# q and k of batches 4 and 5 through the DMA crossbar: a sliding-window attention with a channel mix behind it

## The chip, the core and the metric

The kernel runs on one core of one Trainium2 chip. The metric is the device time of one execution in microseconds (us); the median over several executions is given where there are several. TensorE (PE in the profile, PEld for its weight loads), VectorE (DVE), ScalarE (ACT), GpSimd (POOL) and SyncE (SP) are the core's engines. POOL and SP compute almost nothing here: they issue DMAs.

## The reference, cut to what matters

```python
# q, k, v: 8 batches x 8 heads x 576 positions x 64
scores = scale * q @ k.T                       # per batch and head
bias   = -slope[h] * abs(i - j)                # 0 <= i - j < 128, else masked
attn   = softmax(scores + bias);  a = attn @ v
x      = heads of a side by side               # 8 x 576 x 512
x_prev = x shifted down by one position
xk = mu_k * x + (1 - mu_k) * x_prev;  xr = mu_r * x + (1 - mu_r) * x_prev
k  = relu(xk @ w_k)                            # 512 -> 1024
v  = (k * k) @ w_v                             # 1024 -> 512
out = sigmoid(xr @ w_r) * v
```

## The kernel before, in words

Everything is computed in bf16 with float32 sums. Loads that cast float32 to bf16 are issued by POOL, because only its DMAs cast here.

**Attention** goes batch by batch (b = 0 to 7) and, in a batch, by pairs of heads (g = 0 to 3). For one pair, the first step is q and k with the 64 columns of a head on the partitions: the transposed form. The scores of the whole pair are twelve TensorE matmuls (L728), two ACT exponentials (L742, `at`), two DVE multiplications with a mask that holds the bias (L755). Then come 18 matmuls with v (L783, `attend`), a reciprocal and a multiplication on DVE (L789, L795, `xu`), and a transposition back into `xt`. DVE makes `dl`, `xk` and `xr` from it (L882, L889).

**The channel mix** runs over chunks of 256, 384 or 512 positions of two batches (one chunk spans two of them). A chunk has 8 groups of four matmuls with `wk_sb` (L985), each followed by a ReLU on ACT (L992) and a square on DVE or ACT (L966 and L964, `kk`). Each block of 128 positions then has four matmuls with `wr_sb` (L1003), a tanh on ACT (L1010), two times four matmuls with `wv_sb` (L1019), a product on DVE (L1024, `ot`) and a store on SP's queue (L1049).

**How q and k get transposed** depends on the batch. In all cases the parts up to position 512 go to `cb` (two buffers) and the last 64 positions to `ts`.
- Batches 0 to 2: TensorE, by a finer scheme (L1080, and L1125 and L1128 for the first half of batch 0).
- Batches 3, 4 and 5: `qk_some` takes two pairs of heads at a time: 32 TensorE transpositions of 64 by 64 blocks (L839) into two PSUM buffers of the pool `uno` (four buffers of one bank each), then four ACT copies (L698) of 128 by 512 into `qk`.
- Batches 6 and 7, the members of `XB`: eight DMA transposes on SP's queue (L537, `flip`), one for each 128 positions of q and of k, from `cb` straight into `qx`. TensorE and ACT do nothing for it. `qx` has two buffers; batch 0 uses the same memory for its staging.

The tails in `ts` go through the crossbar for batches 4 to 7 (L630), and `xu` of batches 6 and 7 goes back to `xt` through it too (L904). L839 also serves the way back of batches 1 to 5 (from `xu`).

```python
def flip(b, i, j, g):
    return dma(SPE, FLIP * RATE, FISSUE, lambda e: nc.sync.dma_start_transpose(
        out=qx_buf[xbh[b].idx][:, i, :, 128 * j:128 * j + 128],
        in_=cb_buf[ch[b].idx][:, i, j].rearrange("p h d -> p (h d)")), ...)

# in the loop over batches
if b in XB:
    hq, y = xbh[b], xbl[b]            # all eight flips of the batch
elif g % QM == 0:
    two_q[:] = qk_some(b, g, QM, prio)
```

**The order of the work** is fixed before anything runs. Each operation is a node of a plan, and `ORDER` holds, for PE, ACT and DVE, the complete list of node numbers in which the engine executes them. An engine that waits for one entry executes nothing behind it. POOL's and SP's DMAs are chained in the order in which the program makes them, except that output stores and the `xt` transposes are put among SP's transposes where the planner's clock says; that clock uses the costs in `COST`, a factor for each kind of transfer. The order in POOL's queue is, for each batch: eight loads into `cb` (four of q, four of k), two into `ts`, five of v into `vs` and `tv`.

A store waits on SP for its product on DVE; transposes behind it in the queue wait with it. A load into `cb` waits until the buffer's last reader is done: a TensorE transposition, or a DMA transpose for the batches in `XB`. `ot` has five buffers, of which the planner hands out the lowest free one.

Of the kernel before, what the change touches and what calls it, by code (L numbers as in the profile page):

```python
# [20 lines left out]

ORDER = {
    "PE": [int(x) for x in """
# [16 lines left out]
""".split()],  # L40
    "ACT": [int(x) for x in """
# [12 lines left out]
""".split()],  # L54
    "DVE": [int(x) for x in """
# [16 lines left out]
""".split()],  # L72
}

# [168 lines left out]
def kernel(  # L243
# [14 lines left out]
    B, H, S, D = q.shape  # L258
# [14 lines left out]

    PE, ACT, DVE, POOL, SPE, FAB, VIR = "PE", "ACT", "DVE", "POOL", "SP", "FAB", "VIR"
    NQ, NA, NX, NV, NC = 4, 4, 4, 2, 2
    XB = range(6, B)
    XO = range(6, B)
    X0 = 16
    NWARM = 90
# [16 lines left out]
    WAIT = 0.0  # L296
    START, BACK = 1.7, 0.25
    SKEW = {'v': 0.25, 'tv': 0.3, 'ts': 0.3}
    COST = {'first': 0.9, 'v': 1.2, 'q': 0.944, 'ts': 0.66, 'tv': 0.66, 'w': 0.88, 'run4': 1.0, 'run2': 1.03, 'flip': 1.0, 'mu': 1.0, 'x': 1.0}
    SS = ()  # L300
    OH = range(1, 6)
    QM = 2
# [108 lines left out]
    def fab(queue, us, n, lat, free=(), flip=False):  # L411
        m = max(1, round(us / 0.25))
        us *= COST.get(getattr(n, "kind", None), 1.0)
        n0, edge = n, (n, lat[0])
# [7 lines left out]
    def dma(queue, kb, issue, emit, deps=(), need=(), free=(), lat=(1.0, 0.9), flip=False, kind='x'):  # L422
        n = plan.add(queue, issue, 0.0, list(deps) + [last.get(queue)],
                     (len(plan.nodes),), emit, need)
        n.kind = 'flip' if flip else kind
        last[queue] = n
        if queue == POOL:
            if len(loads) >= 8:
                loads[-8].succ.append((n, 0.9 + BACK))
                n.left += 1  # L430
            y = fab(queue, kb / RATE, n, (START, lat[1] + SKEW.get(kind, 0.0)), free, flip)
            loads.append(y)
            return y
        return fab(queue, kb / RATE, n, lat, free, flip)
# [58 lines left out]
    def issue_t(nd):  # L493
        return 0.53 + 0.00034 * nd
# [35 lines left out]
    def full_load(b, i, h, g):  # L530
        src = (q, k)[i][b, :, 0:SM].rearrange(
            "h (r p) d -> p h r d" if b in XB else "h (p r) d -> p h r d", p=128)
        return [dma(POOL, 256, issue_t(1024), lambda e, r=r: nc.gpsimd.dma_start(  # L533
# [49 lines left out]
    for g, n in ((0, 1), (1, 1), (2, 2)):  # L583
        for i in range(2):
            x = first_load(i, g, n)
# [49 lines left out]
    def batch_load(b, what):  # L635
# [7 lines left out]
        elif what == "b":  # L643
            th[b], tl[b] = tail_load(b)
            if b in XB:
                xbh[b] = Hold("qx")
# [311 lines left out]

    n_hw = 39 + sum(4 if g in FT else 2 for g in range(3)) + 8 * len(XB) + len(XTT) + G * len(XO)
    n_split = -n_hw % 8  # L960
# [282 lines left out]
    for b in range(1, B):  # L1243
# [4 lines left out]
        for g in range(G):  # L1248
            prio = (0, b, 0, g)
            ha = Hold("at")  # L1250
            if b in XB:
                hq, y = xbh[b], xbl[b]
# [77 lines left out]
```

## Time and profile before

| | |
|---|---|
| median of 3 executions | 230.52 us (230.34 to 230.76) |
| the profiled execution | 231.13 us, its span in the trace 229.4 us |
| PE busy | 220.9 us, 96% |
| DVE busy | 187.5 us, 82% |
| ACT busy | 165.6 us, 72% |
| POOL | 92.1 us, 40% |
| granted TensorE clock | full speed throughout |

The profiled execution takes 1.7 us more than the span of its instructions, and is 0.6 us above the median. Busy times of PE are those of pipelined matmuls, whose ends are modelled; the starts of the next instructions tell more than the durations.

### The profile page before, as it was taken

The page shows a single profiled execution, that of the slowest core. Times are in us where ns is not written, and L with a number is a line of the kernel's source. Part 1 is how long each engine was busy: PE and PEld are TensorE (multiplying, and loading weights), DVE is VectorE, ACT ScalarE, POOL GpSimd, SP SyncE. Part 2 cuts the span into 40 slices and gives each one's busy share as a digit, 9 for nine tenths or more (in the row PEclk, how much of TensorE's full clock was granted, in tenths as well). Part 3 has the DMA queues.
Part 4 walks back from the last instruction along what each step waited for, and adds up shares of the span by engine and source line. Part 5 has one row for each costly group of instructions (what it writes and reads, how often), then busy time and mean ns, then how long its engine had stood idle before and what let it go on. Part 6 is the DMA issues. An engine that isn't in the chain of part 4 may idle for free.

```text
span 229.4 us, 6626 instructions
## 1 busy us (share of the span) xinstructions
PE 220.9 (96%) x2681; PEld 134.8 (59%) x2715; DVE 187.5 (82%) x416; ACT 165.6 (72%) x302; POOL 92.1 (40%) x118
## 2 busy tenths in 40 slices
PE   7899999999999999999999999999999999999994
PEld 7485866665756656455655755545675455456542
DVE  6576899899859999979878998999998988864332
ACT  3569999999999989999697757966649434335521
POOL 8757727699954961990004970600000000000000
PEclk9999999999999999999999999999999999999999
DMA  6999999999995999999553999994151133231014
GB/s 166 177 185 199 197 194 178 185 195 167 194 151 114 166 129 195 106 142 137 137 160 77 162 182 147 123 164 150 51 113 49 46 110 87 74 137 47 3 63 166
DMA packets 121279, 31.11 MB, mean 136 GB/s; under 512 B 107929, under 2 KB 117409, under 8 KB 121249
## 3 DMA queue, kind: packets, MB, share of 16 engines
q0 software_dynamic: 95728, 16.26, 93.7%
q1 hardware_dynamic: 23776, 13.84, 23.7%
q10 hardware_dynamic: 1744, 0.59, 1.1%
q8 instruction: 21, 0.34, 0.6%
q14 instruction: 10, 0.07, 0.1%
HBM read 33.56 MB, written 9.44 MB: 187 GB/s over the span
## 4 chain that ended last, share of the span: by engine, by line
PE 87%; ACT 6%; DMA 3%; issue 2%; SPq 1%; DVE 0%; DVEq 0%; ACTq 0%
PE uno L1019 26%; PE uno L985 26%; PE uno L1003 13%; PE duo L728 7%; PE duo L783 7%; DMA qx<-in_q_dram 3%; PE uno L839 3%; ACT at L742 1%; PE uno L689 1%; PE uno L1080 1%; ACT xt L698 1%; ACT kk L964 1%; ACT rl L992 1%; PE duo L715 1%; ACT qk L698 1%
## 5 line engine op out<-in xcount | busy, mean ns | idle before, releaser
L985 PE MATMUL uno<-xk,wk_sb 128*128 128x256 bf16 (+2 forms) x410 | 72.3, 313 | 0.4
L1019 PE MATMUL uno<-wv_sb,kk 128*128 128x512 bf16 (+2 forms) x279 | 67.6, 373 | 1.5 <-issue 1.0
L742 ACT ACTIVATE at<-duo 128x1024 bf16<-128x1024 f32 (+2 forms) x68 | 65.2, 994 | 5.0 <-PE duo L728 4.6
L992 ACT ACTIVATE rl<-uno 128x256 bf16<-128x256 f32 (+2 forms) x104 | 47.7, 478 | 28.5 <-PE uno L985 18.0
L985 PEld LDWEIGHTS <-wk_sb 128*128 128x128 bf16 x416 | 38.4, 97 | 23.3 <-issue 0.8
L502 POOL DMA_DIRECT2D vs<-in_v_dram x32 | 28.3, 896 | 41.6 <-PE duo L783 37.9
L1019 PEld LDWEIGHTS <-kk 128*128 128x128 bf16 x296 | 27.1, 98 | 27.0
L755 DVE TENSOR_TENSOR at<-at,mask 128x1024 bf16<-128x1024 bf16 x56 | 36.9, 681 | 3.0 <-ACT at L742 2.9
L1003 PE MATMUL uno<-wr_sb,xr 128*128 128x512 bf16 x133 | 36.0, 380 | 0.6
L966 DVE TENSOR_TENSOR kk<-rl 128x384 bf16<-128x384 bf16 (+2 forms) x89 | 28.8, 343 | 9.1 <-ACT rl L992 8.8
L1010 ACT ACTIVATE rs<-uno 128x512 bf16<-128x512 f32 x36 | 22.1, 617 | 17.5 <-PE uno L1003 15.6
L1024 DVE SCALAR_TENSOR_TENSOR ot<-rs,uno 128x512 f32<-128x512 bf16 (+2 forms) x37 | 24.3, 669 | 11.8 <-PE uno L1019 9.4
L889 DVE SCALAR_TENSOR_TENSOR xr<-dl,mu_sb,xt 128x576 bf16<-128x576 bf16 (+1 forms) x32 | 24.8, 778 | 0.0
L889 DVE SCALAR_TENSOR_TENSOR xk<-dl,mu_sb,xt 128x576 bf16<-128x576 bf16 (+1 forms) x32 | 24.6, 778 | 0.2
L783 PEld LDWEIGHTS <-at 128*128 128x128 bf16 x576 | 21.4, 97 | 5.2 <-issue 0.3
L795 DVE TENSOR_TENSOR xu<-duo,rc 128x640 bf16<-128x640 f32 x28 | 22.9, 822 | 0.7 <-PE uno L839 0.2
L698 ACT COPY qk<-uno 128x512 bf16<-128x512 bf16 (+1 forms) x41 | 21.9, 586 | 1.0 <-PE uno L1128 0.7
L1003 PEld LDWEIGHTS <-xr 128*128 128x128 bf16 x144 | 13.5, 98 | 13.7
L783 PE MATMUL duo<-vs,at 128*128 128x65 bf16 x448 | 19.1, 193 | 0.1
L533 POOL DMA_DIRECT2D cb<-in_k_dram x20 | 17.8, 933 | 0.6 <-PE duo L783 0.5
L533 POOL DMA_DIRECT2D cb<-in_q_dram x20 | 17.7, 925 | 0.7 <-DMA ts<-in_q_dram 0.6
L698 ACT COPY xt<-uno 128x640 bf16<-128x640 bf16 (+3 forms) x28 | 15.2, 579 | 3.4 <-PE uno L839 1.8
(83 smaller groups left out, 204.2 us busy)
## 6 DMA issues: line engine op xcount, KB each, us to landing
out_dram<-ot SPq DMA_DIRECT2D x30, 256.0 KB, 2.7
vs<-in_v_dram POOLq DMA_DIRECT2D x32, 128.0 KB, 6.6
cb<-in_q_dram POOLq DMA_DIRECT2D x20, 128.0 KB, 6.4
cb<-in_k_dram POOLq DMA_DIRECT2D x20, 128.0 KB, 6.3
out_dram<-ot SPq DMA_DIRECT2D x10, 128.0 KB, 1.8
wk_sb<-in_moe_w_k_dram POOLq DMA_DIRECT2D x2, 512.0 KB, 9.3
cb<-in_q_dram POOLq DMA_DIRECT2D x4, 256.0 KB, 8.7
cb<-in_k_dram POOLq DMA_DIRECT2D x4, 256.0 KB, 8.4
```

Source lines behind the costliest of these rows:

```text
L502: return dma(POOL, 256, issue_t(1024), lambda e: nc.gpsimd.dma_start(out=vs_buf[h.idx][:, j, :, 0:D], in_=v[b, :, 128 * j:128 * j + 128].r ...
L533: return [dma(POOL, 256, issue_t(1024), lambda e, r=r: nc.gpsimd.dma_start(out=cb_buf[h.idx][:, i, r], in_=src[:, :, r]), [g], kind="q") f ...
L698: (nc.scalar.copy if e == ACT else nc.vector.tensor_copy)(out=out, in_=in_)
L742: lambda e, ah=ah, w=w, hp=hp: nc.scalar.activation(out=ah(), in_=two(hp)[:, :, 0:w], func=AF.Exp, scale=float(scale)), (), [hp])
L755: nc.vector.tensor_tensor(out=a, in0=a, in1=m, op=ALU.mult)
L783: nc.tensor.matmul(a[:, hl, t - t0], lhsT=at[:, lo:lo + 128], rhs=vs[:, u, 2 * g + hl, 0:W] if u < NF else tvb[:, 2 * g + hl, 0:W], start= ...
L889: lambda e: nc.vector.scalar_tensor_tensor(out=buf[hk.idx][:, g, e0 + c0:e0 + c1], in0=dls(), scalar=mu[:, g:g + 1], in1=xc(1), op0=ALU.mu ...
L966: nc.vector.tensor_tensor(out=out, in0=in_, in1=in_, op=ALU.mult)
L985: nc.tensor.matmul(one(hp)[:, 0:n], lhsT=wk_sb[:, po, 128 * fo:128 * fo + 128], rhs=xk_buf[hx.idx][:, po, c0:c1], start=(po == 0), stop=(p ...
L992: a = op(ACT, act_t(n), [s], pr, lambda e, hp=hp, hr=hr: nc.scalar.activation(out=rl_buf[hr.idx][:, 0:n], in_=one(hp)[:, 0:n], func=AF.Rel ...
L1003: nc.tensor.matmul(one(hp), lhsT=xr_buf[hx.idx][:, po, 128 * c:128 * c + 128], rhs=wr_sb[:, po], start=(po == 0), stop=(po == NPO - 1))
L1019: nc.tensor.matmul(one(hv)[:, a:b], lhsT=kk_buf[hk.idx][:, fo, o:o + 128], rhs=wv_sb[:, fo, a:b], start=(fo == 0), stop=(fo == NFO - 1))
```

## The change

Batches 4 and 5 join `XB`. Their q and k are loaded into `cb` with 128 consecutive positions on the partitions instead of every fourth, as for batches 6 and 7 (the sizes of the pieces stay), and 16 DMA transposes are added on SP's queue. Four calls of `qk_some` go: 128 TensorE transpositions with their 128 weight loads and 16 ACT copies. Four batches now share the two buffers of `qx`, so the transposes of batches 6 and 7 wait until the scores of batches 4 and 5 have read theirs. The loads into `cb` for batches 6 and 7 now wait for DMA transposes.

The factor for loads of v in the planner's clock becomes 0.98, and all three lists are new ones. Counted over the program, the new lists also give 5 more squares to DVE and 5 fewer to ACT, and 2 copies of batch 0's q and k go from ACT to DVE. The same 90 warm-up matmuls (L689) stand at other places among the first operations of PE. Two lines of the lists fall away, so that line numbers behind them are lower by 2 in the changed kernel.

```diff
 ORDER = {
     "PE": [int(x) for x in """
-76 65 57 55 58 54 39 69 41 49 48 43 75 61 52 47 51 50 45 46 73 68 67 66 63 56 60 70 72 44 71 42 131 40 59 53 74
+105 101 76 85 128 75 52 119 121 46 117 98 47 65 40 51 81 68 97 88 122 84 41 112 48 120 72 93 82 94 77 45 63 100
...
-    XB = range(6, B)
+    XB = range(4, B)
...
-    COST = {'first': 0.9, 'v': 1.2, 'q': 0.944, 'ts': 0.66, 'tv': 0.66, 'w': 0.88, 'run4': 1.0, 'run2': 1.03, 'flip': 1.0, 'mu': 1.0, 'x': 1.0}
+    COST = {'first': 0.9, 'v': 0.98, 'q': 0.944, 'ts': 0.66, 'tv': 0.66, 'w': 0.88, 'run4': 1.0, 'run2': 1.03, 'flip': 1.0, 'mu': 1.0, 'x': 1.0}
```

84 rows, old and new, of the table ORDER are left out of this document.

## The prediction

> **What bounds the kernel now.** I read the page first: busy shares, then the chain that ended last.
>
> ```profile
> span 229.4 us, 6626 instructions
> ...
> PE 220.9 (96%) x2681; PEld 134.8 (59%) x2715; DVE 187.5 (82%) x416; ACT 165.6 (72%) x302; POOL 92.1 (40%) x118
> ...
> PE 87%; ACT 6%; DMA 3%; issue 2%; SPq 1%; DVE 0%; DVEq 0%; ACTq 0%
> ```
>
> TensorE carries 87% of the chain. The averages hide stages, so I cut the span in windows (columns: PE, PEld, DVE, ACT and POOL busy, then clock, DMA share, GB/s).
>
> ```profile
> 30.00:60.00 30.00, 29.45 (x511) 18.72 (x513) 28.18 (x54) 29.35 (x55) 23.29 (x29) 1.00 1.99 187
> 60.00:105.00 45.00, 44.31 (x626) 27.21 (x633) 39.72 (x81) 41.87 (x75) 31.35 (x38) 1.00 1.88 145
> 105.00:150.00 45.00, 44.21 (x532) 26.57 (x540) 40.47 (x84) 34.92 (x60) 16.79 (x20) 1.00 1.29 141
> 150.00:200.00 50.00, 49.69 (x413) 27.64 (x416) 46.57 (x92) 27.57 (x46) 0.00 (x0) 1.00 0.43 92
> ```
>
> From 30 to 200 us PE idles 0.55 + 0.69 + 0.79 + 0.31 = 2.34 us. Up to 60 us DVE (94%) and ACT (98%) are nearly as full; from 105 on ACT has room and DVE becomes the second (93% at the end). So PE's work is the time, with DVE close behind.
>
> **What goes from TensorE.** The four removed calls stand in the timeline of PE as groups of 32 on L839 from `cb`; beside each I show what starts next. The last two rows are scores of batch 1 with a 128-row matmul behind them.
>
> ```profile
> 83.83 0.56 PE L728 MATMUL duo<-qk 64*128 64x256 bf16 x8
> 84.28 0.63 PE L839 MATMUL uno<-ident,cb 64*128 64x64 bf16 x32
> 85.07 0.81 PE L1019 MATMUL uno<-wv_sb,kk 128*128 128x512 bf16 x3 [0.16 <-issue]
> ...
> 89.80 0.63 PE L839 MATMUL uno<-ident,cb 64*128 64x64 bf16 x32
> 90.36 0.63 PE L783 MATMUL duo<-vs,at 128*128 128x65 bf16 x15
> ...
> 103.00 0.63 PE L839 MATMUL uno<-ident,cb 64*128 64x64 bf16 x32
> 103.79 0.38 PE L1019 MATMUL uno<-wv_sb,kk 128*128 128x512 bf16 x1 [0.16 <-issue]
> ...
> 112.45 0.63 PE L839 MATMUL uno<-ident,cb 64*128 64x64 bf16 x32
> 113.25 0.81 PE L1019 MATMUL uno<-wv_sb,kk 128*128 128x512 bf16 x3 [0.16 <-issue]
> ...
> 38.60 0.56 PE L728 MATMUL duo<-qk 64*128 64x256 bf16 x8
> 39.17 1.89 PE L1019 MATMUL uno<-wv_sb,kk 128*128 128x512 bf16 x7
> ```
>
> From start to next start the four take 0.79, 0.56, 0.79 and 0.80: 2.94 us. Three of them follow scores directly, and part of their price comes back: scores to transpositions take 84.28 - 83.83 = 0.45, scores to a 128-row matmul 39.17 - 38.60 = 0.57, so 0.12 stays behind in each. Gain: 2.94 - 3 x 0.12 = **2.58 us**. Bounds: 2.2 (four times 0.56) to 2.94. Nothing covers this work: PE executes its list in order and has next to no gaps there.
>
> **What goes from ACT and comes to DVE.** Groups by shape:
>
> ```profile
> L698 ACT COPY qk<-uno 128x512 bf16<-128x512 bf16 x37 | 20.5, 609 | 0.9 <-PE uno L1128 0.7
> L698 DVE COPY qk<-uno 128x512 bf16<-128x512 bf16 x5 | 3.3, 686 | 0.3 <-ACT kk L964 0.3
> L966 DVE TENSOR_TENSOR kk<-rl 128x256 bf16<-128x256 bf16 x36 | 9.8, 285 | 2.4 <-ACT rl L992 2.3
> ```
>
> ACT loses 16 x 0.609 = 9.7 us of copies and two more copies (1.2). None of that is on the path while PE is full; it frees two of four `uno` buffers earlier, four times. DVE gains 5 x 0.285 + 2 x 0.686 = 2.8 us, all before about 70 us; the window to 60 us leaves it 1.8 us idle. I take 0.2 us as exposed, near the covered end, since PE only waits for DVE by way of buffers; bounds 0 and 2.8.
>
> **What comes to SP.** Sixteen transposes. Their rows, from SP's timeline, and the time from issue to landing (minimum, median, maximum) of DMAs that touch `qx`:
>
> ```profile
> 108.56 6.47 SPq L537 DMA_TRANSPOSE qx<-cb  x5
> ...
> 115.75 2.20 SPq L537 DMA_TRANSPOSE qx<-cb  x1
> ...
> DMA to landing us min/median/max: 2.5/5.3/7.9
> ...
> qx<-cb SPq DMA_TRANSPOSE x16, 4.1
> ```
>
> One occupies the queue for 6.47 / 5 = 1.29 us, at worst 2.20, and lands in 4.1, at worst 7.9. 16 x 1.29 = 21 us of SP, whose queue otherwise waits for products; what matters is whether PE's fixed list waits for them. For positions in the new list I sum TensorE work ahead, with 0.55 for a pair's scores, 0.55 for its `attend`, 0.86 for four 512-wide matmuls (less for narrower ones), from the chain of waits:
>
> ```profile
> 68.82 0.55 PE duo L728 x12
> ...
> 86.43 0.86 PE uno L985 x4
> ...
> 89.02 0.55 PE duo L783 x18
> ...
> 93.67 0.55 PE duo L728 x12
> ```
>
> In the old list 62.2 us of work stands ahead of batch 3's first scores, which start at 68.8, and 86.2 ahead of batch 4's, which start at 93.7: start and gaps add 6.6, later 7.5. In the new list 84.6 stands ahead of batch 4's first scores, so PE gets there at 92. Batch 4's transposes: two are early; the other six stand behind a store whose product needs `wv_sb` matmuls that end at 65.0 + 6.6 = 71.6, so about 72.3 with the product. Then 72.3 + 6 x 1.29 + 4.1 = 84.1, and the tails one transpose later, 85.4. Slack: **6.6 us**. Batch 5, the same way: seven behind a store ready at 94.4, landed by 107.5, tails 109; needed at about 118 (110.3 of work ahead). Batch 6's wait until batch 4's last scores have read `qx` (about 109) and land by about 131, needed at 143; batch 7's by 158, needed at 167. Stores behind a batch's transposes come up to 8 x 1.29 = 10 us later, in front of a pool of `ot` buffers not used up. Price on the path: 0, covered by this slack.
>
> The loads feed them, on POOL's queue:
>
> ```profile
> 71.69 3.53 POOL L502 DMA_DIRECT2D vs<-in_v_dram  x4 [5.00 <-PE duo L783]
> ...
> 79.31 3.58 POOL L533 DMA_DIRECT2D cb<-in_k_dram  x4
> ...
> cb<-in_k_dram POOLq DMA_DIRECT2D x20, 128.0 KB, 6.3
> ...
> 109.00:115.00 6.00, 5.79 (x99) 3.86 (x100) 5.37 (x14) 4.21 (x8) 0.00 (x0) 1.00 0.56 129
> ```
>
> v of batch 4 is issued when batch 2's `attend` is over; that comes 1.3 us later in the new list, so the last load of batch 5 is issued at 84.2 and lands at 90.5. From 109 to 115 five transposes with no load beside them kept the DMA engines 0.56 of the time busy: at most 0.56 x 6 / 5 = 0.67 us each. Batch 4's eight add up to 5.4 us to the loads of batch 5 beside them: 96 instead of 90.5, past 94.4 but within that batch's slack of 9. By the Trainium skill's page DMA: Bandwidth & Descriptors, section Issuing engines are not separate DMA queues, all queues run on the same 16 engines and interleave, which speaks against the change; no row shows transposes and loads at full rate together long enough to price it better than these 5.4 us.
>
> **The start.** The new list puts the first channel-mix groups before most tail scores of batch 0 and has 27 instead of 48 warm-ups after 10 us, which could save about 1 us. But batch 0's `wr_sb` matmuls come at 30.93 in the trace, and POOL's slot of the `wr_sb` load comes free at 30.0:
>
> ```profile
> 8.60 0.98 PE L1125 MATMUL uno<-id,qx 128*128 128x128 f32 x7 [1.02 <-DMA qx<-in_q_dram]
> ...
> 30.02 0.76 POOL L498 DMA_DIRECT2D cb<-in_q_dram  x1 [1.25 <-DMA wr_sb<-in_moe_w_r_dram]
> ...
> 30.93 1.89 PE L1003 MATMUL uno<-wr_sb,xr 128*128 128x512 bf16 x7
> ```
>
> The new list has them 0.5 us of work earlier, at 30.4. A better start than by 0.4 us is lost there again. On the other side, batch 0's second scores now stand behind transpositions that wait for the q load until 8.6 us. I take 0, between -0.4 and +0.5.
>
> **Sum.** -2.58 + 0.2 + 0 = -2.4 us. On the profiled execution's own 231.13 that makes 228.7; it stood 0.6 over the median, so from 230.52 I forecast **228.1 us**. Its own range, by the bounds of the transpositions, of the start and of up to 0.6 on DVE: 227.1 to 229.4.
>
> **Rivals.**
>
> *Late transposes (ends slower).* Place: batch 4's first scores. With 2.20 us each and 7.9 to landing they land at 72.3 + 13.2 + 7.9 = 93.4, already 1.4 late. At 3 us each, with loads on the same engines, 98.2: 6.2 late, and nothing behind can run, so 231.1 + (6.2 - 2.4) on the profile, **234.3** on the median. It decides from about 2.6 us each, where lateness (3.8) passes the gain. For: the single row of 2.20 us, and full DMA engines before 105 us. Against: five in a row at 1.29 us. Chance 0.11.
>
> *DVE becomes the bound.* All of its 2.8 us show: -2.58 + 2.8 = +0.2, **230.7**; with half, 229.3. For: 94% up to 60 us and 93% at the end, where the new list's last `xr` is due 14 us of PE work after the third-last `attend`, with 13 us of DVE work between. Against: PE waits for DVE hardly anywhere now. Chance 0.16.
>
> *More than the work goes.* ACT at 93% between 60 and 105 us and the `uno` buffers cost PE part of the 2.34 us of gaps; if half of them close, 228.1 - 1.2 = **226.9**. Chance 0.11.
>
> *TensorE does not set the time.* Then removing transpositions does nothing: **230.5**. For it speaks PEld at 59%; matmuls overlap, so 96% overstates. The Trainium skill (Perfetto Trace Analysis, section Identifying the Most-Contended Engine) says matmul busy time is a poor measure of headroom for that reason. Against: the starts above follow each other without a gap. Chance 0.03.
>
> **How the numbers follow.** The forecast keeps 0.59. A measurement of this kernel can tell about 0.2% (0.46 us) from no change. Faster: 0.59 + 0.11 + a third of DVE's 0.16 = 0.75. Slower: 0.11 + 0.03 of DVE's = 0.14. Same: the rest of DVE's and PE's case, 0.11. The range of 226.7 to 231.1 holds all but the late transposes, the worst of DVE's case and a little below: about 0.15.
>
> **What would show it.** Right: L839 from `cb` x64; PE busy near 218.5; gaps from 30 to 200 us still about 2.3; transposes of 1.3 us on SP; `qx` landed 6 us before batch 4's first scores. Wrong: a wait of PEld on L726 for a DMA transpose into `qx` (late), gaps of PE with DVE as releaser above 2 us (DVE), or PE busy down by 2.5 and the span unchanged.

## The result, and the profile after

The changed kernel takes 228.86 us (median of 4 runs, 228.72 to 229.10) where the kernel before takes 230.52: ratio 0.9918, 95% interval 0.9893 to 0.9942. It is faster, by 1.66 us; the forecast was 2.4 us, and 228.1 us. The profiled execution of after took 228.84 us with a span of 227.1.

From the page of after (span, busy time, chain by engine), then its windows in the stretches that the prediction used, and all waits of TensorE:

```profile
span 227.1 us, 6442 instructions
...
PE 221.8 (98%) x2587; PEld 133.2 (59%) x2587; DVE 188.8 (83%) x423; ACT 155.0 (68%) x279; POOL 92.0 (41%) x118
...
PE 92%; ACT 3%; DMA 2%; SPq 1%; issue 0%; DVE 0%; DVEq 0%; ACTq 0%
```

```profile
30.00:60.00 30.00, 29.91 (x510) 19.00 (x509) 28.75 (x56) 29.07 (x54) 22.34 (x28) 1.00 1.95 184
60.00:105.00 45.00, 45.00 (x564) 26.30 (x561) 40.60 (x82) 36.62 (x61) 28.40 (x34) 1.00 1.87 159
105.00:150.00 45.00, 45.00 (x479) 25.91 (x477) 39.48 (x81) 30.48 (x52) 19.70 (x24) 1.00 1.80 176
150.00:200.00 50.00, 50.00 (x434) 27.79 (x433) 46.01 (x94) 28.52 (x47) 0.21 (x1) 1.00 0.61 98
```

```profile
PE uno L687 <- DVE warm L469: 1.0, 1, 1.0
PE uno L1123 <- DMA qx<-in_q_dram: 0.5, 1, 0.5
```

TensorE is still the bound, and the list shows no wait of its matmuls behind the first load of q. One thing does not fit the profile of before: PE's busy time rose from 220.9 to 221.8 although 128 matmuls are gone. The counts tell why: before has 2681 matmuls and 2715 weight loads, after 2587 of both. 34 matmul records are missing from the trace of before, and the missing ones look like idle time. The first experiment shows what that did to the prediction.

SP's queue in after, from its timeline, and from the list of DMAs the time from issue to landing over the whole program (median):

```profile
73.00 9.30 SPq L535 DMA_TRANSPOSE qx<-cb  x6
82.47 1.60 SPq L628 DMA_TRANSPOSE tt<-ts  x1
...
94.07 11.06 SPq L535 DMA_TRANSPOSE qx<-cb  x7
105.22 0.54 SPq L1047 DMA_DIRECT2D out_dram<-ot  x1
105.92 1.24 SPq L628 DMA_TRANSPOSE tt<-ts  x1
```

```profile
cb<-in_k_dram POOLq DMA_DIRECT2D x20, 128.0 KB, 12.1
...
qx<-cb SPq DMA_TRANSPOSE x32, 7.5
...
tt<-ts SPq DMA_TRANSPOSE x4, 7.1
```

A transpose takes 9.30 / 6 = 1.55 us of the queue instead of 1.29 and lands after 7.5 instead of 4.1; the loads of k land after 12.1 instead of 6.3. So the transposes are in time by less than was forecast. Below, W means that a removed group is worth 0.46 us, P that it is worth the prediction's 2.58 / 4 = 0.645, and L that the crossbar's transposes are in time only with the new lists.

### The profile page after: what moved, and what is told of

Its sections match the earlier page's. It is cut to its first block, busy times and chain, and to the rows that moved or that the text cites. A ratio compares the mean times of both kernels' runs of the same rounds, so it can differ in the third digit from the quotient of the medians.

```text
span 227.1 us, 6442 instructions
## 1 busy us (share of the span) xinstructions
PE 221.8 (98%) x2587; PEld 133.2 (59%) x2587; DVE 188.8 (83%) x423; ACT 155.0 (68%) x279; POOL 92.0 (41%) x118
## 4 chain that ended last, share of the span: by engine, by line
PE 92%; ACT 3%; DMA 2%; SPq 1%; issue 0%; DVE 0%; DVEq 0%; ACTq 0%
PE uno L983 28%; PE uno L1017 28%; PE uno L1001 13%; PE duo L726 7%; PE duo L781 7%; DMA qx<-in_q_dram 2%; PE uno L837 2%; PE uno L1078 2%; ACT at L740 1%; PE duo L713 1%; ACT qk L696 1%; PE uno L781 1%; SPq L550 1%; PE uno L687 1%; PE uno L820 1%; PE uno L939 0%
## 5 line engine op out<-in xcount | busy, mean ns | idle before, releaser
L1017 PE MATMUL uno<-wv_sb,kk 128*128 128x512 bf16 (+2 forms) x296 | 69.7, 374 | 0.0
L990 ACT ACTIVATE rl<-uno 128x256 bf16<-128x256 f32 (+2 forms) x104 | 46.4, 471 | 26.4 <-PE uno L983 21.0
L964 DVE TENSOR_TENSOR kk<-rl 128x256 bf16<-128x256 bf16 (+2 forms) x94 | 30.2, 339 | 8.8 <-ACT rl L990 8.4
L1008 ACT ACTIVATE rs<-uno 128x512 bf16<-128x512 f32 x36 | 21.1, 604 | 22.2 <-PE uno L1001 22.1
L887 DVE SCALAR_TENSOR_TENSOR xr<-dl,mu_sb,xt 128x576 bf16<-128x576 bf16 (+1 forms) x32 | 24.3, 776 | 0.0
L781 PE MATMUL duo<-vs,at 128*128 128x65 bf16 x448 | 18.6, 193 | 0.0
L880 DVE TENSOR_TENSOR dl<-xt 128x576 bf16<-128x576 bf16 (+1 forms) x32 | 13.5, 432 | 2.8 <-ACT xt L696 2.7
## 6 DMA issues: line engine op xcount, KB each, us to landing
cb<-in_k_dram POOLq DMA_DIRECT2D x20, 128.0 KB, 12.1
```

The lines of the kernel that those rows point to most:

```text
L781: nc.tensor.matmul(a[:, hl, t - t0], lhsT=at[:, lo:lo + 128], rhs=vs[:, u, 2 * g + hl, 0:W] if u < NF else tvb[:, 2 * g + hl, 0:W], start= ...
L887: lambda e: nc.vector.scalar_tensor_tensor(out=buf[hk.idx][:, g, e0 + c0:e0 + c1], in0=dls(), scalar=mu[:, g:g + 1], in1=xc(1), op0=ALU.mu ...
L964: nc.vector.tensor_tensor(out=out, in0=in_, in1=in_, op=ALU.mult)
L990: a = op(ACT, act_t(n), [s], pr, lambda e, hp=hp, hr=hr: nc.scalar.activation(out=rl_buf[hr.idx][:, 0:n], in_=one(hp)[:, 0:n], func=AF.Rel ...
L1017: nc.tensor.matmul(one(hv)[:, a:b], lhsT=kk_buf[hk.idx][:, fo, o:o + 128], rhs=wv_sb[:, fo, a:b], start=(fo == 0), stop=(fo == NFO - 1))
```

## The experiments

**The kernel before, profiled again.** No edit.

> The kernel before, profiled a second time. Theory W (the time is TensorE's work; a removed group of 32 transpositions costs 0.46 us beyond the switch to 128 rows that its neighbour pays anyway, because in three of the four rows the next group shows x3 or x1 instead of x4: its first record, 0.216 us, is missing): the groups behind L839 show 0.57 us to the next start wherever all four records are there, and the span is nearer to 228.8 than to 229.4, because the first profile waited 0.6 us longer for the first q load. Theory P (the prediction's price, 0.64 each): 0.79 again, span 229.4.

It took 230.57 us, span 228.8, with 2715 matmul records for 2715 weight loads. From PE's timeline, the four groups and what starts next, then the windows of this run in the same stretches:

```profile
83.75 0.63 PE L839 MATMUL uno<-ident,cb 64*128 64x64 bf16 x32
84.31 1.04 PE L1019 MATMUL uno<-wv_sb,kk 128*128 128x512 bf16 x4
...
89.27 0.63 PE L839 MATMUL uno<-ident,cb 64*128 64x64 bf16 x32
89.83 0.63 PE L783 MATMUL duo<-vs,at 128*128 128x65 bf16 x15
...
102.47 0.63 PE L839 MATMUL uno<-ident,cb 64*128 64x64 bf16 x32
103.03 1.90 PE L1019 MATMUL uno<-wv_sb,kk 128*128 128x512 bf16 x8
...
111.92 0.63 PE L839 MATMUL uno<-ident,cb 64*128 64x64 bf16 x32
112.49 1.04 PE L1019 MATMUL uno<-wv_sb,kk 128*128 128x512 bf16 x4
```

```profile
30.00:60.00 30.00, 30.00 (x497) 18.66 (x485) 28.27 (x55) 29.50 (x56) 23.30 (x30) 1.00 2.00 188
60.00:105.00 45.00, 45.00 (x637) 27.05 (x636) 39.55 (x81) 41.87 (x75) 30.85 (x37) 1.00 1.88 146
105.00:150.00 45.00, 45.00 (x547) 26.87 (x544) 40.66 (x84) 34.92 (x60) 16.78 (x20) 1.00 1.26 141
150.00:200.00 50.00, 50.00 (x409) 27.42 (x408) 46.23 (x91) 27.45 (x47) 0.00 (x0) 1.00 0.40 92
```

Each group takes 0.56 or 0.57 from start to next start, not 0.79. The matmuls behind the first and the last group are counted x4 here and x3 in the prediction's rows, those behind the third x8 here and x7 in the first trace (the stretch that the prediction shows ends behind one of them): each time the first matmul was a missing record, and the second stood there as "what starts next". And from 30 to 200 us PE is never idle: the 2.34 us of gaps were the missing records too. In this complete trace PE is busy for 223.7 us, so the 221.8 of after are 1.9 less: near four times 0.46 (1.84), and not near 2.58.

**The groups put back.** Sixteen groups of 32 transpositions, of a constant and with results that nobody reads, go into the changed kernel; a run with four of them (behind the condition on four pairs of batches 4 and 5) came first.

```diff
+            if b >= 4:        # first run: if (b, g) in ((4, 1), (4, 2), (5, 0), (5, 3))
+                for i in range(16):
+                    for r in range(2):
+                        nc.tensor.transpose(two(todo[0][5])[:, r]..., dist[...], ident[...])
             if bias:
```

> The changed kernel with four groups of 32 transpositions of a constant put in ahead of four scores of batches 4 and 5; nobody reads their result, and nothing else changes. It prices the TensorE work by itself. Theory W: 228.9 + 4 x 0.46 = 230.7 us. Theory P: 228.9 + 4 x 0.64 = 231.4.

> The changed kernel with sixteen groups of 32 transpositions of 64 by 64 (of a constant, results unread), one in the scores of each pair of batches 4 to 7: the TensorE work of the removed groups, put back four times over. Theory W (0.46 us each): 7.4 us more, 236.2 to 236.6. By the prediction's 2.58 / 4 = 0.645 each: 10.3 more, 239.3.

Measured: 231.2 us with four (ratio to before 1.0015, 1.0001 to 1.0029) and 236.87 with sixteen (1.0236, 1.0205 to 1.0267). PE's timeline of the run with sixteen, the first group:

```profile
91.73 0.63 PE L713 MATMUL duo<-ident,dist 64*128 64x64 bf16 x32
92.19 0.55 PE L733 MATMUL duo<-qx 64*128 64x256 bf16 x8
```

0.46 us from start to next start. Over the program, TensorE's last group of matmuls shows the same, first in the second trace of the changed kernel (below), then in the run with sixteen:

```profile
222.58 1.26 PE L1017 MATMUL uno<-wv_sb,kk 128*128 128x384 bf16 x12
```

```profile
230.59 1.26 PE L1024 MATMUL uno<-wv_sb,kk 128*128 128x384 bf16 x12
```

It starts 8.01 us later. Of that, 0.64 is there at batch 1's first scores already (29.60 instead of 28.96), ahead of any group, for a reason that was not followed, and (8.01 - 0.64) / 16 = 0.46. That is W; the median of 236.87 is 0.3 above W's range, less than the 0.64 of the start. The four alone add 1.8 behind the start (0.45 each) and 2.2 in the medians, between W and P; the sixteen decide.

**The changed kernel again, and with three transposes more.** The second run puts three further DMA transposes of batch 4's q, into memory that nobody reads, ahead of the last of its eight.

```diff
+            if (b, i, j) == (4, 1, NF - 1):
+                for t in spare:
+                    nc.sync.dma_start_transpose(out=t, in_=cb_buf[ch[b].idx][:, 0, 0]...)
             nc.sync.dma_start_transpose(
                 out=qx_buf[xbh[b].idx][:, i, :, 128 * j:128 * j + 128], ...
```

> The changed kernel once more, beside the ones that follow. Theory W (the four groups are worth 0.46 us each, 1.84 in all, next to nothing else moved): 228.6 to 229.1 us, ratio to the kernel before 0.991 to 0.994; matmul rows complete, no idle time of TensorE above 0.3 us behind the first q load; the last transpose for batch 4 lands about 1.5 us ahead of its first scores. Theory P (the prediction's 2.58 us): 228.1.

> The changed kernel with three more DMA transposes of batch 4's q, into spare memory that nobody reads, put ahead of the last of batch 4's eight on SP's queue. At 1.55 us each, as the trace of the changed kernel has them, they push the last transpose and the tails behind it back by about 4.6 us. Theory W (they land 1.5 us ahead of their need): batch 4's first scores wait 2.5 to 3.5 us on the tails or on qx, and the time rises by as much, to 231.3 to 232.4. By the prediction's slack of 6.6 us: no wait, 228.9. If a wait there were made up later: a wait of some us in the trace and a time under 230.

The changed kernel: 229.02 us, ratio 0.9927 (0.9905 to 0.9949), span 227.1. Its transpose of the tails is issued at 82.64 and lands 7.3 us later (median), at 89.9; they are read at 91.5. With three transposes more: 235.15 (median of six; the ratio of 1.0176, 1.0134 to 1.0219, is that of five, without the longest), the profiled execution 233.07. PE's timeline there:

```profile
91.48 0.49 PE L733 MATMUL duo<-qx 64*128 64x256 bf16 x6
94.45 0.23 PE L733 MATMUL duo<-qx 64*128 64x128 bf16 x2 [2.47 <-DMA qx<-cb]
95.42 0.20 PE L733 MATMUL duo<-tt,qx 64*128 64x64 bf16 x2 [0.73 <-DMA tt<-ts]
```

The tails are issued 4.7 us later (87.34), and PE waits 2.47 + 0.73 = 3.2 us at batch 4's first scores and starts its last group 3.9 us later, 0.3 of it from the start on. So 4.7 us more became 3.2 to 3.6 us of delay, and the slack was 1.1 to 1.5 us by this run, 91.5 - 89.9 = 1.6 by the trace without the three: not 6.6. W expected 231.3 to 232.4 us; it came out at 233.1 in the profiled execution, with a granted clock of 0.998, and at 234.5 to 236.6 in the five others, with 0.984 to 0.992. In those five a late transpose cost more than its wait; a later experiment shows where the rest may go.

**The old lists.** Batches 4 and 5 through the crossbar, but in the order of before, without the entries that fall away. One run keeps the planner's factor for v at 1.2, the second has 0.98, so that it differs from the changed kernel in the lists alone.

```diff
-    XB = range(6, B)
+    XB = range(4, B)
-    COST = {..., 'v': 1.2, ...}
+    COST = {..., 'v': 0.98, ...}        # second run only
```

> The crossbar for batches 4 and 5 alone: the old lists and the old cost factor, with only the four groups and their 16 copies taken out. Theory W: 230.5 - 1.8 = 228.7 us. Theory P: 230.5 - 2.6 = 227.9. Theory L (the new lists are needed, since the old ones let TensorE reach batch 4's or 5's scores before the transposes have landed): 229.5 or more, with a wait of TensorE at the first scores of batch 4 or 5.

> Batches 4 and 5 through the crossbar with the old operation lists, without the entries that fall away, and with the planner's factor for v of the change (0.98), so that its only difference from the changed kernel is the lists. With the factor of before (1.2) it took 233.1, with a wait of 1.9 us for the tails of batch 5. Theory L (the lists themselves decide): 232 to 233.5, a wait of 1 to 2 us for a transpose at batch 5's scores remains. Rival F (the factor, which puts the stores among the transposes, made the wait): under 230.5 and no wait of TensorE for a DMA above 0.5 us behind 20 us.

Measured 233.12 (ratio 1.0102, 1.0069 to 1.0135) and 235.40 (1.0186, 1.0158 to 1.0214): slower than before, both. The first one's PE timeline at batch 5, then the longest waits of PE in the second:

```profile
111.78 0.56 PE L725 MATMUL duo<-qx 64*128 64x256 bf16 x8
114.26 0.20 PE L725 MATMUL duo<-tt,qx 64*128 64x64 bf16 x2 [1.92 <-DMA tt<-ts]
```

```profile
PE uno L982 <- DVE ot L1021: 3.2, 2, 2.1
PE duo L725 <- DMA tt<-ts: 1.4, 1, 1.4
```

L holds: batch 5's tails come late, by 1.9 and 1.4 us. In the first run that is not the whole price: from 30 to 200 us PE idles 3.2 us in its trace, and none in the second trace of before; the 1.3 us beside the tails are smaller waits that were not followed. The first run has batch 4's first scores at 93.5 and batch 5's at 111.8; the changed kernel has batch 4's earlier (91.1 instead of 93.5) and batch 5's later (117.4), which is where its tails, issued at 105.9 and 7.1 us on the way, need to be. The factor 0.98 did not help the old lists: PE then waits 3.2 us for products into `ot`, and these wait for earlier stores to be done with the buffer that the planner gave them. The product at 119.31 waits 4.70 us that way; the last store ahead of it, issued at 113.76, lands 5.4 us later, at 119.2. How the factor led to that was not followed, and L had not expected it: 235.4 is above its 232 to 233.5.

**The new lists without the crossbar.** Batches 4 and 5 back on TensorE; I put the four groups and their 16 ACT copies into the new lists.

```diff
-    XB = range(4, B)
+    XB = range(6, B)
     # ORDER: 4 entries more for PE, 16 for ACT
```

> The new lists alone: q and k of batches 4 and 5 on TensorE again, four groups of 32 transpositions and 16 copies put back into the new lists at places like the old ones. Theory W: 228.9 + 1.8 = 230.7 us. Theory P: 228.9 + 2.6 = 231.5, so that the new lists by themselves cost 0.9. Theory L: near 230.5 as well, but only together with a slow kernel of old lists and crossbar.

243.08 us (1.0517). PE waits for ACT where I put the copies (2.6 us for one copy into `qk`, 1.7 and 1.5 for copies into `xt`), and its granted clock falls as well, to 0.52 from 90 to 92 us. So this run tells of my places more than of the lists, and what the lists give by themselves stays open. It does show that at these places the lists have little room for ACT's copies. The next run measures that.

**ACT's copies put back as mere work.** Sixteen ACT copies of 128 by 512 of a constant, read by nobody, behind the exponentials of batches 4 and 5 of the changed kernel.

```diff
-                out=ah(), in_=two(hp)[:, :, 0:w], func=AF.Exp, ...), (), [hp])
+                ...Exp...) if b not in (4, 5) else (
+                ...Exp..., nc.scalar.copy(out=spare, in_=dist[:, 0:512])), (), [hp])
```

> The changed kernel with 16 further ACT copies of 128 by 512 (of a constant, into spare memory), one behind each exponential of batches 4 and 5: 16 x 0.61 = 9.7 us of ACT, as much as the change took away. Theory W and the prediction alike (ACT's copies were off the path): 228.9 to 229.3. Rival A (relief of ACT is part of the gain): 229.6 or more, with waits of TensorE for ACT that add up to over 0.5 us.

231.89 us (1.0023, 1.0007 to 1.0040), against 229.13 for a run of the changed kernel with lighter loads on the same chip (next experiment): 2.8 us more. The traces say the same: TensorE's last group starts at 225.53 instead of 222.58 in the changed kernel's second trace, 2.95 later, 0.2 of it from the start on. Windows of the changed kernel, then of this run, from 91 to 111 us (PE, PEld, DVE, ACT, POOL busy):

```profile
91.00:111.00 20.00, 20.00 (x209) 11.44 (x203) 18.29 (x37) 15.61 (x26) 11.19 (x14) 1.00 1.91 171
```

```profile
91.00:111.00 20.00, 18.97 (x183) 10.14 (x182) 17.08 (x34) 16.88 (x30) 11.76 (x14) 1.00 1.99 160
```

Here rival A holds, against W and the prediction alike. Six of the sixteen copies lie in this stretch (each takes 0.63 us, 10.1 in all), and PE falls behind: the scores at 91.16 in the changed kernel start 0.40 later here, those at 108.02 start 2.00 later. PE waits 0.57 us for a ReLU and 0.22 for a copy into `xt`, and gets through 183 matmuls instead of 209, though ACT is only 84% busy. So ACT's work is on the path at these places, as a delay of what PE waits for next; the two waits are half of the 1.6 us, and the rest was not followed. It does not say that the removal of the copies brought time by itself: in the order of before they stood at other places, and the only wait of PE for ACT that its second trace lists is one of 0.2 us.

**Lighter loads beside the transposes.** Batch 5's loads of q and k, which run beside batch 4's transposes, are cut to one head of eight; a second run adds the three extra transposes.

```diff
-            out=cb_buf[h.idx][:, i, r], in_=src[:, :, r]), ...
+            out=cb_buf[h.idx][:, i, r, 0:n], in_=src[:, 0:n, r]), ...   # n = 1 if b == 5 else H
```

> The changed kernel, with the loads of batch 5's q and k cut to one head of eight (the same number of DMAs, an eighth of their bytes and rows; batch 5's results are not the reference's). They run on POOL's queue beside batch 4's eight transposes. Theory C (the loads beside them make the transposes late): batch 4's six transposes in a row take 1.2 to 1.3 us each instead of 1.55 to 1.62, land after 2.5 to 5 us instead of 8.6, and the tails after 3 to 5 instead of 7.3; the time stays 228.8 to 229.2, since the transposes already land in time. Rival S (the transposes slow each other, or the stores do): 1.5 us each and 7 to 9 us to landing, as with the loads.

> The three extra transposes of the run before and the cut loads of batch 5 together (batch 5's results are not the reference's). Theory C: without the loads beside them all eleven transposes and the tails land by about 88, ahead of 91.2, so no wait of TensorE for a DMA at batch 4's scores, and the time is 228.9 to 229.5 instead of 233 and more. Rival S: the wait of 2 to 3 us stays, 232 to 235.

Measured 229.13 (0.9914, 0.9880 to 0.9948) and 229.85 (0.9941, 0.9917 to 0.9965). From 69 to 82.4 us, DMAs issued and POOL's traffic (q0: packets, MB, and the time of its packets as a share of 16 engines' time, which passes 100% where packets overlap), in the changed kernel and with lighter loads:

```profile
q0 software_dynamic: 4822, 0.61, 89.3%
...
qx<-cb SPq DMA_TRANSPOSE x8, 8.6
```

```profile
q0 software_dynamic: 5342, 0.67, 86.0%
...
qx<-cb SPq DMA_TRANSPOSE x8, 5.9
```

Half of theory C. The transposes land after 5.9 instead of 8.6 us, six in a row take 1.34 each instead of 1.62, and the three extra ones now cost TensorE no wait in the profiled execution (228.95 us, span 227.2) where they cost 3.2. That execution is the fastest of nine; the median of 229.85 is above C's 229.5. And the transposes do not fall to the 2.5 to 5 us that C expected, because q0 moved as much in that stretch as before: it is mostly v of batch 4 (four loads of 128 KB and one of 64), which the edit leaves alone. The kernel before itself holds the cleaner pair. From 110 to 120 us, then from 130 to 140, in its second trace:

```profile
q1 hardware_dynamic: 3567, 1.31, 53.7%
...
qx<-cb SPq DMA_TRANSPOSE x6, 2.9
```

```profile
q0 software_dynamic: 9365, 1.18, 209.1%
q1 hardware_dynamic: 1171, 0.57, 24.4%
...
qx<-cb SPq DMA_TRANSPOSE x2, 7.0
```

In the first stretch POOL's queue moves nothing and six transposes land in 2.9 us; in the second it is full and two transposes take 7.0, with fewer transposes and no store beside them: against rival S. The other direction shows in the run with three transposes more: batch 5's four loads of k land after 15.0 us (median), in the changed kernel's second trace after 12.6. The 4.1 us of the prediction was a median over both kinds, and the places where batches 4 and 5 need theirs are all of the second kind.

**One batch more.** Batch 3 through the crossbar too.

```diff
-    XB = range(4, B)
+    XB = range(3, B)        # lists: those of the change without the entries that fall away
```

> Batch 3 too goes through the crossbar; two further groups of 32 TensorE transpositions and eight ACT copies fall away, the lists of the change otherwise as they are. If its eight transposes landed in time, W gives 228.86 - 2 x 0.46 = 227.9 and P 227.6. But its loads are issued until 52.4 us beside those of batch 4, at 1.55 us each eight transposes take 12.4 us, and 7 to 9 us pass to landing, against a need at 69.2: theory W expects a wait of 1 to 4 us at batch 3's first scores and a time of 229 to 232, no gain on the changed kernel. By the prediction's figures (1.29 us each, 4.1 to landing) they would land 5 us earlier, by about 67, and the time be 227.6.

238.02 us (1.0325, 1.0297 to 1.0352): much slower. PE waits for batch 3's `qx` at every pair of heads, then works at a granted clock of 0.50 (the first wait and the next full run of matmuls in PE's timeline, then windows; the clock is the third number from the end):

```profile
PE duo L726 <- DMA qx<-cb: 6.1, 4, 2.6
```

```profile
71.48 0.28 PE L726 MATMUL duo<-qx 64*128 64x256 bf16 x2 [2.61 <-DMA qx<-cb]
...
76.34 1.89 PE L1017 MATMUL uno<-wv_sb,kk 128*128 128x512 bf16 x4
```

```profile
71.00:72.00 1.00, 0.28 (x2) 0.10 (x2) 0.09 (x1) 0.00 (x0) 0.31 (x1) 0.99 1.71 156
72.00:76.00 4.00, 0.79 (x4) 0.21 (x4) 0.00 (x0) 1.02 (x1) 0.00 (x0) 0.50 1.73 184
76.00:78.00 2.00, 1.98 (x10) 0.82 (x11) 0.00 (x0) 1.02 (x1) 0.00 (x0) 0.50 1.55 171
78.00:79.00 1.00, 1.00 (x4) 0.40 (x3) 0.67 (x2) 0.00 (x0) 0.00 (x0) 0.60 1.75 154
79.00:80.00 1.00, 1.00 (x23) 0.80 (x21) 0.23 (x2) 0.00 (x0) 0.10 (x1) 1.00 2.40 156
```

W had expected 229 to 232 and a wait of 1 to 4 us. The wait was 6.1, and the granted clock fell to 0.50 from 72 until about 78.8, some 2.5 us of that with PE busy again (its next full run of matmuls starts at 76.3). The Trainium skill (TensorE: Matmul & The Clock Gate, section HAM oscillation — how this bites in real kernels) says that an idle gap of TensorE of more than about 3.4 us brings its clock down, and that the work behind the gap then starts at the low clock. The second half agrees with this trace. The first does so only roughly: the clock fell 3.1 us after PE had run out of work at 68.9, with 0.28 us of work in between and no single wait above 2.6 us. The same may be the rest of the run with three extra transposes, whose longer executions had mean clocks of 0.984 to 0.992; those were not traced, so that is argued and not shown.

## Why the prediction was right, and where it was wrong

It had the mechanism and the sign: TensorE's work was the time, the removed groups were on its path, the transposes were in time with the new lists, and nothing else took their place. The range of 226.7 to 231.1 also held 230.5, no change at all, so the number alone says little. Point by point:

- **TensorE's term, 2.58 us, was mis-sized.** The step that failed is "from start to next start the four take 0.79, 0.56, 0.79 and 0.80". Three of them were lengthened by a missing record. With 0.56 each and 0.12 that stays behind in all four (the one at 89.80 follows other 64-row transpositions, so its switch stays as well) the term is 4 x 0.44 = 1.76, or 1.84 by the 0.46 that the sixteen groups showed. Even the lower bound of 2.2 was too high. 230.52 - 1.8 = 228.7 is within 0.2 of what was measured.
- **DVE's exposed 0.2 us and the start's 0** cannot be told apart from nothing: after has no wait of TensorE for DVE beyond the warm-up, DVE grew by 1.5 us (187.3 to 188.8) and not 2.8, and batch 1's first scores come at 28.98 instead of 29.13 in the second trace of before, 0.15 earlier.
- **ACT's relief, "None of that is on the path while PE is full",** was right for the order of before, and is not a property of ACT: in the new order 10.1 us of copies on ACT cost 2.8 us.
- **The slack of 6.6 us was wrong, the price of 0 right.** PE's need at 92 was good (91.1). The failing terms are 1.29 us each (1.55), taken from a stretch without loads beside, and 4.1 to landing (7.1 to 8.6), a median over stretches with and without. The slack was 1.1 to 1.6 us. With the measured figures the prediction's own sum gives 72.3 + 7 x 1.55 + 7.3 = 90.5 for the tails, against its 92: still in time, but by a margin that it did not know. That the price stayed 0 is in part luck. The estimate that transposes would delay loads by up to 5.4 us is borne out in direction (loads of k 12.1 instead of 6.3 at the median), but the reverse, loads that delay transposes, was not in the sum. By the Trainium skill's page DMA: Bandwidth & Descriptors, section Issuing engines are not separate DMA queues, all queues interleave on the same engines. These rows agree, in both directions.
- **The rivals.** Late transposes were the real danger, nearer than a slack of 6.6 us made them look: the old lists gave 233.1 and 235.4 and three extra transposes 235.2, near its 234.3. (Its sum has a slip: lateness passes the gain of 2.4 from 2.4 us each, not 2.6.) "More than the work goes" had nothing to stand on, as the gaps that it was to close were missing records; PE busy near 218.5 and gaps of still 2.3 us failed as signs for the same reason (221.8; 0.1 from 30 to 200 us). DVE did not become the bound.
- **What stays open:** what the new lists give by themselves, and a quarter of a microsecond between 1.84 with the start's 0.15 and the 1.7 that TensorE's last group shows (it starts at 224.27 in the second trace of before, at 222.56 in after).

## What to carry to other kernels

Count matmuls against weight loads before reading starts and gaps: where records are missing, the gap behind a group is longer than the work, and a second trace costs less than a wrong term. A transfer's time to landing is to be taken from a stretch with the same traffic beside it, not from a median over the program. When work moves from a full engine to DMA, the order of the operations decides whether it pays: the same change was worth -0.8% with one list and +1.0% to +1.9% with another.

## What was not expected of the hardware

- Transposes and cast loads slow each other: transposes land after 2.9 us with no load beside, after 7.0 to 8.6 beside loads; loads of k after 6.3 us in the kernel before, 12.1 in the changed one, while loads of q stay at 6.3 in its first trace and take 10.2 in its second (medians).
- A late transfer can cost TensorE twice: with waits of 6.1 us for one batch the granted clock fell to 0.50 for over 6 us, and the kernel lost 9 us in all (229.0 to 238.0). Waits of 2.5 and 0.7 us left it at full speed in the one traced execution that had them.
- ACT at 68% of the span (78% from 91 to 111 us) is no room at every place: 10.1 us of copies between 93.7 and 146 us cost 2.8 us.
